# Load order of the late weights in a fused attention and feed-forward kernel: down weights ahead of output weights, gate weights split two and five

## The chip, the cores and the metric

The kernel runs on one core of a Trainium2 chip. The metric is the device time of one execution in microseconds (us), lower is better; times are medians over several runs.

## The reference

One transformer block with parallel branches over 2048 tokens of width 448: a layer norm, a sliding-window attention of 16 heads of 28 (window 256), a gated feed-forward of width 1792, and the sum of both with the input. All tensors are bf16.

```python
def _A_ref(x, wqkv, wo):
    qkv = (x @ wqkv).reshape(B, S, 3, H, Dh) ...            # H = 16, Dh = 28
    scores = einsum("bhqd,bhkd->bhqk", q, k) * Dh ** -0.5
    mask = (idx[:, None] - idx[None, :] >= 0) & (idx[:, None] - idx[None, :] < 256)
    p = softmax(where(mask, scores, -1e9))
    return einsum("bhqk,bhkd->bhqd", p, v) ... @ wo

def _B_ref(x, w_gate, w_up, w_down):
    return (gelu(x @ w_gate) * (x @ w_up)) @ w_down

xn = layernorm(x)
return x + _A_ref(xn, A_wqkv, A_wo) + _B_ref(xn, B_w_gate, B_w_up, B_w_down)
```

## The kernel before

**Tiling.** The tokens are cut into four query blocks of 512 (`qb` 0 to 3), each of four tiles of 128. For a block, `attention` runs the score steps (score matmuls into a PSUM tile of four banks, an exponential on ScalarE, masks, then the product with the values), and between the steps it runs pieces of other matmul work from a hand-written list, `plan`: projections of the next block, up-projections of this one, and the down and output projections of the block before (`gen_down`). After the attention steps of a block `gated` runs the feed-forward: the hidden width of 1792 is taken as seven pairs of 128 columns (pair p is columns 128p to 128p+127 of each half). For each pair `gate(p)` makes 14 matmuls into a PSUM tile `gt` of two banks and a GELU of 1024 columns on ScalarE (L539), `up(p)` makes the 14 matmuls of the up-projection, and `end(p)` multiplies both on VectorE (L546, L549) and calls `hook(2p)`. Block 0 makes the up-projection of pairs 0 to 4 ahead of time, in the attention steps, so that its `gated` runs gate 0 to 4, then gate 5, up 5, gate 6, up 6.

**PSUM.** The `gt` tiles are two buffers of two banks, the score tile `sc` of the next block is one buffer of all four of those banks. So the first score matmul of block 1 waits for the last GELU of block 0, and the second score step for the exponential of the first.

**Order.** The schedule is by hand: every engine runs its instructions in the order in which the code issues them. SyncE's queue (SP) issues nearly all DMAs. Eight DMA semaphores (HW0 to HW7, "lanes" below) are used in turn by the DMAs of SP and of ScalarE's queue, in program order. A DMA that is to use a lane first waits until the DMA that used it eight DMAs earlier has landed.

**The loads in question.** `ahead3` runs in the third score step of block 0. It issues, on SP, the copies `swap` and `swap_weights`, the gate weights `wg` with `load_ffn` (a load is two DMAs, one for each half of the partitions), the last two pairs of the up weights `wu`, the last four input tiles (`x_sb`, L827), the output weights `wo` in eight small DMAs (L831, L832) and the down weights `wd` in two large ones (L834). The last four rows of each head group in `wo` are laid out by `SLOTS`, since heads 14 and 15 travel in spare rows.

**What uses them.** `gate(p)` reads `wg`; `gen_down(0)`, in the attention steps of block 1, reads `wd` (L408) and later `wo` (L408, L417). The `wo` rows 64 to 127 of group 3 are a copy of rows 0 to 63, made on GpSimd (Pool) in `hook`. `hook` of block 0 also calls, at f = 8 (the end of pair 4), `o_collect(0, nc.scalar)`: three DMAs on ScalarE's own queue (L364) that take the attention output of heads 14 and 15 to DRAM, after Pool has written it (L622). At f = 0, 4, 8 and 10 it normalises an input tile (L170) and has SP transpose it by DMA (L184); at f = 12 `o_deliver` (L369) brings the rows back and Pool copies a part (L375).

Of the kernel before, what the change touches and what calls it, by code (L numbers as in the profile page):

```python
# [19 lines left out]
NF = F // P  # L20
# [7 lines left out]
def kernel(  # L28
# [11 lines left out]
    nc = tc.nc  # L40
# [26 lines left out]
    wg = const.tile([P, 7, F // 2], bf16, name="wg")  # L67
    wu = const.tile([P, 7, F // 2], bf16, name="wu")
    wd = const.tile([P, NF, D], bf16, name="wd")
    wo = const.tile([P, 4, D], bf16, name="wo")  # L70

    def rows(w, c0, n):
        return w[c0 * P:(c0 + n) * P, :].rearrange("(c p) n -> p c n", p=P)

    def load_ffn(dst, w, pairs):

        wv64 = w.rearrange("(c p) (h n) -> p c h n", p=64, h=2)
        ns = slice(pairs.start * P, pairs.stop * P)  # L80
        for hi in range(2):
            nc.sync.dma_start(out=dst[64 * hi:64 * hi + 64, :, ns], in_=wv64[:, :, hi, ns])
# [82 lines left out]
    def norm(t):  # L165
        xn = work.tile([P, 4, P], bf16, name="xn", bufs=4)
        xf = xn[:, :, :].rearrange("p a b -> p (a b)")
        both = ((0, D, 0), (D, 64, 384))
        for lo, n, src in both if t > 3 else both[:1]:
            nc.vector.tensor_scalar(out=xf[:, lo:lo + n], in0=x_sb[:, t, src:src + n], scalar1=mv_all[:, t, 0:1],  # L170
                                    scalar2=rstd_all[:, t:t + 1], op0=ALU.subtract, op1=ALU.mult)
        xns[t] = xn
# [9 lines left out]
    def dma_transp(t):  # L182

        nc.sync.dma_start_transpose(out=xnT[:, :, t * P:(t + 1) * P], in_=xns.pop(t)[:, :, :].rearrange("p a b -> p (a b)"))  # L184
# [103 lines left out]
    def fill_pads(last):  # L288


        def put(dst, src, n, lo):

            src = src.rearrange("p (j d) -> p j d", d=Dh)[:, :, lo:]
            if n == 4:
                nc.gpsimd.tensor_copy(out=dst[:, 12:16, Dh:32], in_=src[:, :, 24:28])
            src = src[:, :, 0:24].rearrange("p j (g i) -> p g j i", i=8)[:, :, :, 0:4]
            nc.gpsimd.tensor_copy(out=dst[:, 0:12, Dh:32].rearrange("p (g j) i -> p g j i", j=4), in_=src)

        if not last:
            for c in range(3):  # L300
                k = wraw[:, c, D + 12 * Dh:2 * D]
                put(wqp[:, c, :, :], k, 4, 0)
                put(wkp[:, c, :, :], k, 3, 4)
            return
        put(w3p[0:64, :, :], w3k[0:64, :], 4, 0)
        put(w3p[64:128, :, :], w3k[64:128, :], 3, 4)
        nc.gpsimd.memset(w3p[64:128, 12:16, :], 0.0)
# [163 lines left out]
    def new_hT(qb):  # L471
        hT = blk.tile([P, NF, QB], bf16, name="hT", tag="hT")
        hTs[qb] = hT

    def swap(qb, t=None, n=4):

        t0 = P * (4 * qb if t is None else t)
        to = t0 - qb * QB + ring(qb).start
        for hi in range(2):
            nc.sync.dma_start(out=xsw[64 * hi:64 * hi + 64, :, to:to + n * P],  # L480
                              in_=xnT[64 - 64 * hi:P - 64 * hi, 0:3, t0:t0 + n * P])

    def swap_weights():

        for hi, src in enumerate((wqp, wkp)):
            nc.sync.dma_start(out=wsq[64 * hi:64 * hi + 64], in_=src[64 - 64 * hi:P - 64 * hi, 0:3])
# [19 lines left out]
    def gen_up(qb, ps, shared=()):  # L506

        for p in ps:
# [9 lines left out]
            yield 330  # L518

    def gated(qb, early, last_v, flush, hook):  # L520

        hT = hTs[qb]
# [293 lines left out]
    def ahead3():  # L816
        for t in (5, 6, 7):
            norm(t)
            dma_transp(t)
        swap(1, 4, 2)  # L820
        fill_pads(False)
        swap_weights()
        swap(1, 6, 2)
        load_ffn(wg, B_w_gate, slice(0, 3))
        load_ffn(wg, B_w_gate, slice(3, 7))
        load_ffn(wu, B_w_up, slice(5, 7))
        nc.sync.dma_start(out=x_sb[:, 12:16, :], in_=xv[:, 12:16, :])  # L827
        wo_v = A_wo.rearrange("(g j d) n -> j d g n", g=4, j=4)
        tail = A_wo[14 * Dh:, :].rearrange("(t i) n -> i t n", i=4)
        for j, (t0, n) in enumerate(SLOTS):  # L830
            nc.sync.dma_start(out=wo[32 * j:32 * j + Dh, 0:n, :], in_=wo_v[j][:, 0:n])  # L831
            nc.sync.dma_start(out=wo[32 * j + Dh:32 * j + 32, 0:n, :], in_=tail[:, t0:t0 + n])  # L832
        for k in range(0, NF, 7):
            nc.sync.dma_start(out=wd[:, k:k + 7, :], in_=rows(B_w_down, k, 7))  # L834

    for qb in range(NB):
        if qb in (1, 3):
            tc.mark_branch_hint_location("general", hint="LikelyTaken",
                                         engines=[mybir.EngineType.DVE if qb == 1 else mybir.EngineType.PE])
        early = ()  # L840
        if qb == 0:
            new_hT(0)
            early = (0, 1, 2, 3, 4)
            def last_v():
                v_dense(2, pvs[2], False)
                v_copy(2, pvs[2], nc.vector.tensor_copy)

            u = chain(gen_qk(), gen_up(0, (1, 2, 3, 0, 4), (2, 3, 4)))
            w = gen_pairs(1, (("v", 0), ("v", 2), ("k", 0), ("k", 1), ("k", 2)))
            plan = [[last_v, lambda: stat(6), (u, 3), ahead], [(u, 2), ahead2, (u, 2)], [(u, 1), ahead3, (u, 7)], [(u, 8), lambda: stat(8)],  # L850
                    [lambda: stat(9), (u, 12), lambda: fill_pads(True)], [(u, 9), "sums"],
                    [(w, 7), "inverse", "scale", (w, 7), lambda: stat(10), (w, 3)],
                    [(w, 4), lambda: stat(11), lambda: rstd(8, 4), (w, 7), "masks", "sums", (w, 7), "inverse"]]
        else:
            d = gen_down(qb - 1)
            if qb < 3:
                u = gen_pairs(qb + 1, (("v", 0), ("k", 0), ("v", 2), ("k", 1), ("k", 2)))
                plan = [[(d, 14)], [(d, 11)], [(d, 11)], [(u, 7)], [(d, 17)], ["sums", (d, 1), (u, 7), "inverse"], [(u, 11)],
                        [lambda: q_last(qb + 1, nc.vector.tensor_copy), (d, 6), "sums"], [(d, 2), "inverse", (d, 9)],
                        [(u, 9), "masks", (u, 1)]]  # L860
                plan[3] = [(d, 1), (u, 7)]
                if qb == 2:
                    plan[0], plan[2] = [(d, 13)], [(d, 10)]
                if qb == 1:
                    for i, j in enumerate((0, 1, 2, 2)):
                        plan[j].insert(0, lambda t=12 + i: stat(t))
                    plan[4].append(lambda: rstd(12, 4))
                    plan[1] = plan[1][:1] + [lambda: q_last(1, nc.vector.tensor_copy), (d, 8)]
                    plan[2] = plan[2][:2] + [(d, 12), lambda: collect(1)]
                    plan[4].append(lambda: deliver(1))  # L870
            else:
                new_hT(3)
                early = (1, 2, 3, 4, 5, 6)
                u = gen_up(3, early, (4, 5, 6))
                plan = [[(u, 12)], [(u, 9)], [(d, 12)], [(d, 10)], [(d, 12)], [(d, 1), (u, 7), "sums"], [(d, 12), "inverse"],
                        ["sums", "inverse", (d, 11)], [(d, 11)], [(d, 1), "masks", (u, 13), "masks", (u, 1)]]
        if qb in (1, 2):
            swap(qb + 1)
        score_pool(1)
        rest, after, flush = attention(qb, plan)  # L880
        nc.scalar.preload_act_table(ACT.Gelu_apprx_tanh)
        score_pool(2)
        if qb not in hTs:
            new_hT(qb)

        def hook(f):
            after(f)
            if qb in (1, 2) and f == 0:
                collect(qb + 1)
            if f == (8, 2, 2, 0)[qb]:  # L890
                o_collect(qb, nc.sync if qb else nc.scalar)
            if f == (12, 4, 4, 0)[qb]:
                o_deliver(qb)
                o_finish(qb)
            if qb == 0 and f == 6:
                nc.gpsimd.tensor_copy(out=wo[64:128, 3, :], in_=wo[0:64, 3, :])
            if qb in (1, 2) and f == 10:
                deliver(qb + 1)
            t = ({0: 8, 4: 9, 8: 10, 10: 11} if qb == 0 else {4: 12, 6: 13, 8: 14, 10: 15} if qb == 1 else {}).get(f)
            if t is not None:  # L900
                norm(t)
                dma_transp(t)

        gated(qb, early, rest, flush, hook)
        if qb < NB - 1:
            nc.scalar.preload_act_table_set("natural_log_exp_and_others")
# [159 lines left out]
```

## Time and profile before

| | |
|---|---|
| median of 3 runs | 211.83 us (211.72 to 211.97) |
| the profiled execution | 211.66 us, its span 209.8 us |
| TensorE matmul (PE) busy | 205.4 us, 98% of the span |
| VectorE (DVE) busy | 156.4 us, 75% |
| ScalarE (ACT) busy | 134.7 us, 64% |
| GpSimd (POOL) busy | 44.0 us, 21% |
| DMA | 15.68 MB, 75 GB/s over the span |
| gate weights of block 0 first used | at 36.2 us |
| down weights first used | at 51.4 us |
| output weights first used by PE | at 58.5 us |

The profiled execution took 1.8 us more than its span; that part lies outside what the profile shows. All times below are microseconds from the span's start. Busy time of PE is modelled at the ends of matmuls, so a gap on PE is better read from the start times of its instructions.

### The profile page before, as it was taken

To read this page: it belongs to the slowest core of one execution; us is meant where nothing else is said; L and a number is where in the kernel's file an instruction comes from. 1 tells how busy PE (TensorE), PEld (TensorE's weight loads), DVE (VectorE), ACT (ScalarE), POOL (GpSimd) and SP (SyncE) were. 2 spreads that over 40 slices of the span, in tenths; PEclk is the share of its full clock that TensorE was granted. 3 is DMA by queue.
4 is the path that set the end of the run, shared out by engine and by line. 5 is a ranking of instruction groups with operands and counts; after the bars stand their busy time and mean duration, and the time that the engine had idled before them with its cause. 6 is when DMAs were issued, how large, how long until landed. Compare 5 with 4: busy or idle time off the path is not lost. (4 is left out here: it accounts for less than half of the span.)

```text
span 209.8 us, 6671 instructions
## 1 busy us (share of the span) xinstructions
PE 205.4 (98%) x2842; PEld 98.9 (47%) x2842; DVE 156.4 (75%) x359; ACT 134.7 (64%) x132; POOL 44.0 (21%) x87
## 2 busy tenths in 40 slices
PE   7999999999999999999999999999999999999994
PEld 2444444544454545444445444544444454544572
DVE  6898899899788984796438897395385699696532
ACT  4699896857677977423777787522587787756000
POOL 5389902260000220040000102012000022042000
PEclk9999999999999999999999999999999999999999
DMA  6999989969421001003321000100000010100011
GB/s 171 291 223 212 127 212 217 215 199 221 112 67 25 25 22 22 7 5 70 72 75 47 25 3 25 22 3 21 23 5 0 3 47 5 47 9 13 3 47 50
DMA packets 24890, 15.68 MB, mean 75 GB/s; under 512 B 9208, under 2 KB 24728, under 8 KB 24856
## 3 DMA queue, kind: packets, MB, share of 16 engines
q1 hardware_dynamic: 23814, 14.87, 31.2%
q10 hardware_dynamic: 1042, 0.34, 0.9%
q8 instruction: 23, 0.38, 0.8%
q14 instruction: 11, 0.09, 0.2%
HBM read 9.26 MB, written 2.41 MB: 56 GB/s over the span
## 5 line engine op out<-in xcount | busy, mean ns | idle before, releaser
L687 ACT ACTIVATE p_sb<-sc 128x2048 bf16<-128x2048 f32 x38 | 71.4, 1878 | 16.9 <-PE sc L682 11.9
L539 ACT ACTIVATE p_sb<-gt 128x1024 bf16<-128x1024 f32 x28 | 28.7, 1025 | 31.3 <-PE gt L499 30.2
L622 POOL TENSOR_TENSOR oN<-oc,l 128x512 bf16<-128x512 f32 x16 | 20.7, 1298 | 122.8 <-DVE l L635 122.8
L499 PE MATMUL gt<-xnT,wg 64*128 64x512 bf16 x224 | 45.6, 376 | 0.0
L408 PE MATMUL po<-wd,hT 128*128 128x448 bf16 (+1 forms) x224 | 44.7, 347 | 0.0
L499 PE MATMUL gt<-xsw,wg 64*128 64x512 bf16 x168 | 40.7, 376 | 0.0
L607 DVE TENSOR_TENSOR p_sb<-p_sb,masks 128x256 bf16<-128x256 bf16 (+1 forms) x98 | 30.9, 369 | 7.5 <-ACT p_sb L687 7.5
L549 DVE TENSOR_TENSOR hT<-p_sb,u 128x512 bf16<-128x512 bf16 x34 | 21.7, 675 | 13.4 <-PE u L499 13.3
L408 PEld LDWEIGHTS <-hT 128*128 128x128 bf16 x238 | 21.9, 98 | 19.1 <-issue 2.0
L499 PEld LDWEIGHTS <-wg 64*128 64x128 bf16 x392 | 19.0, 94 | 22.3
L499 PEld LDWEIGHTS <-wu 64*128 64x128 bf16 x392 | 19.1, 94 | 22.0 <-issue 0.7
L499 PE MATMUL u<-xnT,wu 64*128 64x512 bf16 x136 | 28.1, 376 | 0.0
L499 PE MATMUL u<-xsw,wu 64*128 64x512 bf16 x102 | 24.7, 376 | 0.0
L499 PE MATMUL ue<-xnT,wu 64*128 64x512 bf16 x88 | 18.1, 377 | 0.0
L641 DVE TENSOR_TENSOR oc<-oc,ov 128x512 f32<-128x512 f32 (+1 forms) x16 | 10.5, 659 | 9.8 <-ACT oc L639 9.6
L499 PE MATMUL ue<-xsw,wu 64*128 64x512 bf16 x66 | 16.2, 377 | 0.0
L682 PE MATMUL sc<-qT,kT 28*64 28x320 bf16 (+4 forms) x736 | 16.2, 259 | 0.0
L396 DVE TENSOR_TENSOR res<-po,x_sb 128x448 bf16<-128x448 f32 (+1 forms) x14 | 8.1, 606 | 7.9 <-PE po L408 6.7
L682 PEld LDWEIGHTS <-kT 28*64 28x64 bf16 x736 | 8.1, 103 | 12.2 <-issue 11.0
L516 DVE CAST hT<-ue 128x512 bf16<-128x512 f32 x16 | 10.6, 687 | 2.1 <-PE ue L499 2.0
L639 ACT COPY oc<-ov 128x512 f32<-128x512 f32 x16 | 9.4, 585 | 3.6 <-PE ov L656 3.6
L635 DVE STREAM_TRANSPOSE l<-inv_all 128x512 f32<-128x512 f32 x16 | 11.1, 701 | 0.1
(112 smaller groups left out, 256.6 us busy)
## 6 DMA issues: line engine op xcount, KB each, us to landing
out_dram<-res SPq DMA_DIRECT2D x15, 112.0 KB
wd<-in_B_w_down_dram SPq DMA_DIRECT2D x2, 784.0 KB
x_sb<-in_A_x_dram SPq DMA_DIRECT2D x3, 448.0 KB
xsw<-xnT SPq DMA_DIRECT2D x6, 192.0 KB
wu<-in_B_w_up_dram SPq DMA_DIRECT2D x4, 224.0 KB
wg<-in_B_w_gate_dram SPq DMA_DIRECT2D x2, 448.0 KB
wu<-in_B_w_up_dram SPq DMA_DIRECT2D x2, 336.0 KB
wg<-in_B_w_gate_dram SPq DMA_DIRECT2D x2, 336.0 KB
```

What stands on the lines that cost most here:

```text
L408: nc.tensor.matmul(po[:, 0:w], lhsT=x[:, k, tt * P:(tt + 1) * P], rhs=wt[:, k, lo:up], start=start and n == 0, stop=stop and n == len(term ...
L499: nc.tensor.matmul(ps, lhsT=w[64 * hi:64 * hi + 64, c, p * P:(p + 1) * P], rhs=xchunk(qb, hi, c, qb * QB, QB), start=c == 0, stop=c == 6, ...
L516: copy(out=hTs[qb][:, p + 7 * i, :], in_=us[i])
L539: nc.scalar.activation(out=ges[p][:, :, :], in_=gt[:, :, :], func=ACT.Gelu_apprx_tanh)
L549: nc.vector.tensor_tensor(out=hT[:, p + 7 * i, :], in0=ge[:, i, :], in1=u, op=ALU.mult)
L607: nc.vector.tensor_tensor(out=reg, in0=reg, in1=m, op=ALU.mult)
L622: nc.gpsimd.tensor_tensor(out=oN[:, g, :], in0=oc[:, :], in1=inv, op=ALU.mult)
L635: nc.vector.transpose(out=l1[:, :, :], in_=inv_all[:, 4 * qb + g, :].unsqueeze(2).to_broadcast([P, 16, 32]))
L639: nc.scalar.copy(out=oc[:, :], in_=ov[0][:, :])
L641: nc.vector.tensor_tensor(out=oc[:, q0:], in0=oc[:, q0:], in1=ov[1][:, q0:], op=ALU.add)
L682: nc.tensor.matmul(ss[k0:k0 + nk, j, col:col + nq], lhsT=kT[r, g, kt * P + k0:kt * P + k0 + nk], rhs=qT[r, g, ring(qb).start + q0:ring(qb) ...
L687: nc.scalar.activation(out=p_sb[:, :, 0:ncol], in_=ss[:, :, 0:ncol], func=ACT.Exp, scale=SCALE)
```

## The change

The gate weights are loaded as pairs 0 to 1 and pairs 2 to 6 instead of pairs 0 to 2 and 3 to 6. The two DMAs of the down weights are issued ahead of the eight of the output weights. The Pool copy within `wo` is issued at f = 10 instead of f = 6.

```diff
-        load_ffn(wg, B_w_gate, slice(0, 3))
-        load_ffn(wg, B_w_gate, slice(3, 7))
+        load_ffn(wg, B_w_gate, slice(0, 2))
+        load_ffn(wg, B_w_gate, slice(2, 7))
         load_ffn(wu, B_w_up, slice(5, 7))
         nc.sync.dma_start(out=x_sb[:, 12:16, :], in_=xv[:, 12:16, :])
+        for k in range(0, NF, 7):
+            nc.sync.dma_start(out=wd[:, k:k + 7, :], in_=rows(B_w_down, k, 7))
         wo_v = A_wo.rearrange("(g j d) n -> j d g n", g=4, j=4)
         tail = A_wo[14 * Dh:, :].rearrange("(t i) n -> i t n", i=4)
         for j, (t0, n) in enumerate(SLOTS):
             nc.sync.dma_start(out=wo[32 * j:32 * j + Dh, 0:n, :], in_=wo_v[j][:, 0:n])
             nc.sync.dma_start(out=wo[32 * j + Dh:32 * j + 32, 0:n, :], in_=tail[:, t0:t0 + n])
-        for k in range(0, NF, 7):
-            nc.sync.dma_start(out=wd[:, k:k + 7, :], in_=rows(B_w_down, k, 7))
...
-            if qb == 0 and f == 6:
+            if qb == 0 and f == 10:
                 nc.gpsimd.tensor_copy(out=wo[64:128, 3, :], in_=wo[0:64, 3, :])
```

On SP's queue, from the load of the last input tiles to the first DMA transpose of the next block, the rows before are these (a row is one DMA with its line, what it writes and reads, its shape, and the lanes and engines that it waits for; the lane that it waits for is the one that it then uses):

```order
L827 DMA x_sb<-in_A_x_dram 128x4x448 [waits DMAHW0_49]
L831 DMA wo<-in_A_wo_dram 28x4x448 [waits DMAHW1_49,PE_49]
L832 DMA wo<-in_A_wo_dram 4x4x448 [waits DMAHW2_49]
L831 DMA wo<-in_A_wo_dram 28x4x448 [waits DMAHW3_49]
L832 DMA wo<-in_A_wo_dram 4x4x448 [waits DMAHW4_49]
L831 DMA wo<-in_A_wo_dram 28x3x448 [waits DMAHW5_49]
L832 DMA wo<-in_A_wo_dram 4x3x448 [waits DMAHW6_49]
L831 DMA wo<-in_A_wo_dram 28x3x448 [waits DMAHW7_49]
L832 DMA wo<-in_A_wo_dram 4x3x448 [waits DMAHW0_49]
L834 DMA wd<-in_B_w_down_dram 128x7x448 [waits DMAHW1_49]
L834 DMA wd<-in_B_w_down_dram 128x7x448 [waits DMAHW2_49]
L184 DMA_TRANSPOSE xnT<-xn 128x4x128 [waits DMAHW3_49,DVE_49]
```

On the same queue at the same place, the rows of the changed kernel are these:

```order
L827 DMA x_sb<-in_A_x_dram 128x4x448 [waits DMAHW0_49]
L829 DMA wd<-in_B_w_down_dram 128x7x448 [waits DMAHW1_49]
L829 DMA wd<-in_B_w_down_dram 128x7x448 [waits DMAHW2_49]
L833 DMA wo<-in_A_wo_dram 28x4x448 [waits DMAHW3_49,PE_49]
L834 DMA wo<-in_A_wo_dram 4x4x448 [waits DMAHW4_49]
L833 DMA wo<-in_A_wo_dram 28x4x448 [waits DMAHW5_49]
L834 DMA wo<-in_A_wo_dram 4x4x448 [waits DMAHW6_49]
L833 DMA wo<-in_A_wo_dram 28x3x448 [waits DMAHW7_49]
L834 DMA wo<-in_A_wo_dram 4x3x448 [waits DMAHW0_49]
L833 DMA wo<-in_A_wo_dram 28x3x448 [waits DMAHW1_49]
L834 DMA wo<-in_A_wo_dram 4x3x448 [waits DMAHW2_49]
L184 DMA_TRANSPOSE xnT<-xn 128x4x128 [waits DMAHW3_49,DVE_49]
```

The two `wd` rows have moved ahead of the eight `wo` rows, and each `wo` DMA now has a lane two further on: lanes HW5, HW6 and HW7 belonged to the fifth, sixth and seventh `wo` DMA and now belong to the third, fourth and fifth. From the transposes on the lanes are as before.

On ScalarE, from the last copy of attention output of block 0 (L639) to the first exponential of block 1 (L687), the rows are the same before and after; L539 is a GELU, L364 is one of the three DMAs of `o_collect`, L906 loads the function table of the exponential:

```order
L639 COPY oc<-ov 128x512 [waits PE_49,Pool_49]
L539 ACTIVATE p_sb<-gt 128x1024 [waits PE_49] x4
L364 DMA o_130<-oN 28x512 [waits DMAHW5_49,Pool_49]
L364 DMA o_130<-oN 16x512 [waits DMAHW6_49]
L364 DMA o_130<-oN 12x512 [waits DMAHW7_49]
L539 ACTIVATE p_sb<-gt 128x1024 [waits DVE_49,PE_49,Activation_49]
L539 ACTIVATE p_sb<-gt 128x1024 [waits DVE_49,PE_49]
L906 ACT_TABLE_LOAD
L687 ACTIVATE p_sb<-sc 128x2048 [waits DVE_49,PE_49,Activation_49]
```

No row moved here, but the lanes HW5, HW6 and HW7 that the three DMAs wait for are held by other `wo` DMAs than before. On PE the order of instructions is the same too; the wait for the second load of gate weights now stands at the first weight load of gate 2 instead of gate 3, and the first `wo` matmul waits for one lane more. On Pool the order is the same: between f = 6 and f = 10 it has no other instruction.

## Prediction

> **What bounds the kernel now.** I read the page's engine totals first, then the waits, then the order of time on SP, ACT and PE around the moved loads. The page and the waits (waiter, releaser, total, times, longest) say:
>
> ```profile
> PE 205.4 (98%) x2842; PEld 98.9 (47%) x2842; DVE 156.4 (75%) x359; ACT 134.7 (64%) x132; POOL 44.0 (21%) x87
> PEld L682 <- issue: 11.0, 29, 0.4
> PEld L333 <- DMA xsw<-xnT: 0.2, 1, 0.2
> ```
>
> PE is busy for 205.4 of 209.8 us. What it is short of is mostly its own issue between kinds of matmul (29 times, never over 0.4 us); of the DMAs the rows show one wait of 0.2 us. So no load that is moved here is late today, and a gain has almost nothing to come from. What the change can do is make something late. I look for the nearest edges. On PE, around the end of block 0 and the first steps of block 1:
>
> ```profile
> 40.39 0.59 PE L499 MATMUL gt<-xsw,wg 64*128 64x512 bf16 x2
> ...
> 51.05 0.42 PE L682 MATMUL sc<-qT,kT 28*64 28x320 bf16 x16
> 51.41 2.82 PE L408 MATMUL po<-wd,hT 128*128 128x448 bf16 x14
> 54.16 0.43 PE L682 MATMUL sc<-qT,kT 28*64 28x320 bf16 x24
> ```
>
> 40.39 is the start of gate 2, 51.05 the first score step of block 1, 51.41 the first use of `wd`, 54.16 the second score step. On SP, the issue of the loads (start, duration with any wait in the queue):
>
> ```profile
> 31.62 2.94 SPq L827 DMA_DIRECT2D x_sb<-in_A_x_dram  x1
> 34.66 2.20 SPq L831 DMA_DIRECT2D wo<-in_A_wo_dram  x1
> ...
> 39.12 0.32 SPq L831 DMA_DIRECT2D wo<-in_A_wo_dram  x1
> 40.24 0.25 SPq L832 DMA_DIRECT2D wo<-in_A_wo_dram  x1
> 41.13 0.32 SPq L831 DMA_DIRECT2D wo<-in_A_wo_dram  x1
> 42.61 0.25 SPq L832 DMA_DIRECT2D wo<-in_A_wo_dram  x1
> 42.91 1.00 SPq L834 DMA_DIRECT2D wd<-in_B_w_down_dram  x2
> 45.71 6.69 SPq L184 DMA_TRANSPOSE xnT<-xn  x4
> ...
> SPq L831 <- DMA wg<-in_B_w_gate_dram: 1.2, 1, 1.2
> SPq L832 <- DMA x_sb<-in_A_x_dram: 1.1, 1, 1.1
> SPq L832 <- DMA wu<-in_B_w_up_dram: 0.8, 1, 0.8
> SPq L831 <- DMA wu<-in_B_w_up_dram: 0.6, 1, 0.6
> ```
>
> The fifth to eighth `wo` DMA each wait for the lane of an earlier load, so their starts tell when those landed: the last of `wg` at 39.12, the two of `wu` at 40.24 and 41.13, `x_sb` at 42.61, in the order of issue. `x_sb` alone took 2.94 us to be issued, with no wait named: the queue was full. What is issued behind these loads is moved behind them.
>
> **The change, part by part.**
>
> *The down weights.* They may now be issued from 34.66 on, as the queue takes them, and move once `x_sb` has landed at 42.61. Sizes, and the rate of DMA in single microseconds (the last two columns are the DMA share and GB/s):
>
> ```profile
> wd<-in_B_w_down_dram SPq DMA_DIRECT2D x2, 784.0 KB
> x_sb<-in_A_x_dram SPq DMA_DIRECT2D x3, 448.0 KB
> wo<-in_A_wo_dram SPq DMA_DIRECT2D x2, 98.0 KB
> wo<-in_A_wo_dram SPq DMA_DIRECT2D x2, 14.0 KB
> ...
> 36.00:37.00 1.00, 1.00 (x12) 0.58 (x10) 1.00 (x4) 1.00 (x3) 0.00 (x0) 1.00 1.20 218
> 38.00:39.00 1.00, 1.00 (x74) 0.85 (x63) 0.64 (x2) 0.68 (x2) 0.22 (x1) 1.00 1.15 238
> 39.00:40.00 1.00, 1.00 (x12) 0.43 (x10) 0.70 (x2) 1.00 (x2) 1.00 (x1) 1.00 1.15 343
> 41.00:42.00 1.00, 1.00 (x12) 0.49 (x10) 1.00 (x3) 0.61 (x1) 0.00 (x0) 1.00 0.26 62
> 46.00:47.00 1.00, 1.00 (x12) 0.48 (x10) 1.00 (x2) 0.15 (x1) 0.69 (x1) 1.00 1.09 379
> 48.00:49.00 1.00, 1.00 (x12) 0.43 (x10) 1.00 (x3) 0.24 (x1) 0.00 (x0) 1.00 1.14 391
> ```
>
> The two `wd` DMAs are 1568 KB, 1.61 MB. At the mean of their own rate (385 GB/s, from 379 and 391) they take 4.2 us; at the pace of `x_sb` (448 KB from 41.13 to 42.61, 303 KB a us) 5.2 us. So `wd` lands at 46.8 to 47.8. PE wants it at 51.41 and does not wait for it today: gain nothing.
>
> *The output weights.* They now land behind `wd`. The third `wo` DMA lands after 98 + 14 + 98 = 210 KB more, 0.55 to 0.7 us: at 47.35 to 48.5. PE wants `wo` only in the first third of block 1's steps, some ten microseconds on. But ScalarE's queue waits for it: the first DMA of `o_collect` uses the lane HW5, which the fifth `wo` DMA held before (issued at 39.12, landed long ago) and the third holds now. Behind it in ACT's order stand the GELU of gate 5, that of gate 6, the table load and the first exponential of block 1:
>
> ```profile
> 45.68 1.42 ACTq L364 DMA_DIRECT2D o<-oN  x3
> 47.22 1.02 ACT L539 ACTIVATE p_sb<-gt 128x1024 bf16<-128x1024 f32 x1 [1.07 <-POOL wo L896]
> 49.66 1.02 ACT L539 ACTIVATE p_sb<-gt 128x1024 bf16<-128x1024 f32 x1 [1.41 <-PE gt L499]
> 50.70 1.28 ACT L906 ACT_TABLE_LOAD   x1
> 51.99 1.88 ACT L687 ACTIVATE p_sb<-sc 128x2048 bf16<-128x2048 f32 x1
> ...
> 44.38 1.26 POOL L622 TENSOR_TENSOR oN<-oc,l 128x512 bf16<-128x512 f32 x1 [0.36 <-DVE l L635]
> 45.71 0.98 POOL L896 COPY wo<-wo 64x448 bf16<-64x448 bf16 x1
> ```
>
> Today `o_collect` starts at 45.68, when Pool's L622 is done (44.38 + 1.26 = 45.64). From that start to the end of the GELU of gate 5 it is 47.22 + 1.02 - 45.68 = 2.56 us. The GELU of gate 6 starts at 49.66 for PE's sake, so a start of `o_collect` up to 49.66 - 2.56 = 47.10 costs nothing. From there on GELU, table load and exponential have no gap between them, and the exponential ends at 51.99 + 1.88 = 53.87; the second score step, which needs the one score buffer, starts at 54.16. That is at most 0.29 us more. So from 47.10 to 47.39 on, each microsecond of lateness is one on PE, which never makes it up, since it is busy to the end.
>
> The middle of 47.35 and 48.5 is 47.9: 0.5 us past 47.39. The ends: nothing (47.35 is before it) and 1.4 us (48.5 against 47.10). I take 0.5 us, with the middle, since the row of `wd` itself speaks for the fast end and the landing of the load just ahead of it for the slow one.
>
> *The gate weights.* The bytes of both loads together are the same, so the second ends at 39.12 as before; it is now wanted by gate 2 (40.39, its weights some 0.2 us earlier) instead of one gate later. 1.1 us of cover: nothing. The shorter first load frees nobody, since no row has PE waiting for `wg`.
>
> *Pool's copy.* Its place in Pool's order is the same (nothing stands between f = 6 and f = 10), so the edit as such does nothing; what moves it is the lanes it waits for, from 45.71 to about 48. Its successor on Pool is far off:
>
> ```profile
> 55.23 0.40 POOL L375 COPY oN<-oN 64x256 bf16<-64x256 bf16 x1 [8.54 <-DMA oN<-o]
> 45.60 1.64 DVE L546 TENSOR_TENSOR hT<-p_sb,hT 128x1024 bf16<-128x1024 bf16 x2
> 47.68 1.28 DVE L546 TENSOR_TENSOR hT<-p_sb,hT 128x1024 bf16<-128x1024 bf16 x2
> ```
>
> Beside the copy two products of VectorE took 1.64 us, without it 1.28: the 0.36 us are lost two microseconds later instead. Nothing, at most 0.4 either way on DVE, which PE does not wait for by more than that.
>
> *The transposes.* The first now waits on SP for the first `wo` DMA (lane HW3), until about 47.5 instead of 45.71. Four of them and their waits took 6.69 us, to 52.40. At worst they end a microsecond or two later; behind them on SP is `o_deliver`, whose rows Pool copies at 55.23 and PE uses some 3 us after that. That cover hides it; gone, it would cost what exceeds 3 us.
>
> *Waits on PE.* Two more lane waits, at gate 2 and at the first `wo` matmul. Each existing one took 51 ns:
>
> ```profile
> L408 PEldq EVENT_SEMAPHORE  x9: 51/51/51, 51.1 to 198.4; - x9
> ```
>
> Between nothing and 0.1 us together; I take nothing, since they stand in the sequencer, ahead of the matmuls.
>
> *Sum.* 211.66 us of the profiled execution plus 0.5 is 212.16. The median of the runs is 0.17 us above that execution, so I forecast 212.3 us.
>
> **The rivals.**
>
> *It is absorbed: 211.8 us.* In the row 41 to 42 DMA moved only 62 GB/s although `x_sb` landed at 42.61: most of it was there by 41, and a small part trailed by some 1.6 us. If `wo` does not depend on that trailing part, or it catches up, `wd` and three `wo` DMAs follow from 41 on: 41 + 4.2 + 0.55 is 45.8, and `o_collect` starts as it does today. For it: the trailing part would have bandwidth to itself at the end. Against: four landings in a row, 39.12 to 42.61, keep their distance. [...]
>
> *DMA is slower there: 215 us.* If `wd` moves at the pace of the gate weights (228 GB/s, the mean of 218 and 238) it takes 7.0 us and the three `wo` DMAs 0.95: 50.6, 3.2 us past 47.39. Against: the rows from 39 on (343, 379, 391) are of the same shape of load.
>
> *Gate 2 waits: 212.6 us.* If the longer rows of the second load move worse, and it lands after 40.2 instead of 39.12, PE stands at gate 2. The second load has 224 KB more; if the shorter first load gives nothing back, that is 1.0 us at 228 GB/s, 40.1, just in time; 2 us would cost 0.8.
>
> *Something gets faster: 211.2 us.* Earlier `wd` would help if PE waited for it; no row says so.
>
> **How the numbers follow.** The forecast has 0.50 and spans 211.8 to 213.2 (0 to 1.4 us over the median); 0.2%, about what a measurement of this kernel can tell from no change, is 0.42 us, and about a quarter of this case lies below it (0.13). Absorbed 0.32, slow DMA 0.08, gate 2 0.05, faster 0.05. Slower: 0.37 + 0.08 + 0.05 = 0.50. Same: 0.13 + 0.32 = 0.45. Faster: 0.05. The range, 211.7 to 213.3, takes in the absorbed case and all of the forecast; left out are slow DMA and faster.
>
> **What would show it.** Right: in ACT's order of time L364 starts at 47.4 to 48.5 instead of 45.68, the second GELU after it starts later than 49.66, and PE has a gap ahead of the second score step (54.16) and none before. Wrong: L364 still starts by 47.1 (absorbed); a gap on PE at gate 2; PE waiting for `wd` or `wo` itself; or a delay on VectorE that reaches PE at 51.41 first.

## The result and the profile after

The changed kernel is slower. Its median is 213.39 us (22 runs, 211.79 to 216.13), that of the kernel before in the same comparison 211.88 us (22 runs, 211.60 to 214.28). The ratio of the runs that the comparison keeps is 1.0051, with a 95% interval of 1.0028 to 1.0073. The profiled execution took 212.00 us, its span is 210.3 us (211.66 and 209.8 before): it is one of the fastest runs of this kernel, so its rows show the least of the loss. Two more profiles of the same kernel are among the experiments.

The engine totals of the page hardly differ:

```profile
PE 205.1 (98%) x2837; PEld 98.8 (47%) x2842; DVE 156.1 (74%) x359; ACT 134.6 (64%) x132; POOL 44.4 (21%) x87
```

PE's order of time at the same places (gate 2, the first score step, the first use of `wd`, the second score step):

```profile
40.41 0.59 PE L499 MATMUL gt<-xsw,wg 64*128 64x512 bf16 x2
...
51.42 0.42 PE L682 MATMUL sc<-qT,kT 28*64 28x320 bf16 x16 [0.27 <-ACT p_sb L539]
51.78 2.82 PE L408 MATMUL po<-wd,hT 128*128 128x448 bf16 x14
54.61 0.43 PE L682 MATMUL sc<-qT,kT 28*64 28x320 bf16 x24
```

Gate 2 stands where it stood (40.39). The first score step is at 51.42 instead of 51.05 and now waits, for a GELU on ScalarE; the second is at 54.61 instead of 54.16. So 0.37 us are lost at the first and 0.08 more at the second, 0.45 in all, and PE keeps that to the end: it is nearly the whole difference of the two spans (210.3 against 209.8). Behind it stands ScalarE's queue:

```profile
47.76 1.54 ACTq L364 DMA_DIRECT2D o<-oN  x3
49.43 1.94 ACT L539 ACTIVATE p_sb<-gt 128x1024 bf16<-128x1024 f32 x2 [3.26 <-DVE xn L170]
51.39 1.28 ACT L906 ACT_TABLE_LOAD   x1
52.68 1.88 ACT L687 ACTIVATE p_sb<-sc 128x2048 bf16<-128x2048 f32 x1
```

`o_collect` starts at 47.76 instead of 45.68, and the two GELUs, the table load and the exponential follow without a gap, 0.7 us late. (The releaser that the row names, L170, is not it: the GELU starts at 49.43, behind the three DMAs ahead of it in the queue, which end at 49.30.) The wait for the first lane, HW5, is an instruction of its own on this queue, and is over at 47.4, before at 45.1; `o_collect` itself starts almost 0.4 us behind it:

```profile
L364 ACTq EVENT_SEMAPHORE  x1: 17/17/17, 47.4 to 47.4; - x1
```

On SP the reason:

```profile
32.69 5.81 SPq L829 DMA_DIRECT2D wd<-in_B_w_down_dram  x2
...
43.70 0.32 SPq L833 DMA_DIRECT2D wo<-in_A_wo_dram  x1
46.90 0.25 SPq L834 DMA_DIRECT2D wo<-in_A_wo_dram  x1
47.24 6.26 SPq L184 DMA_TRANSPOSE xnT<-xn  x4
...
SPq L834 <- DMA wd<-in_B_w_down_dram: 2.9, 1, 2.9
```

The seventh and the eighth `wo` DMA wait for the lanes of the two halves of `wd`: these landed by 43.70 and 46.90. The first transpose waits for the first `wo` DMA, and starts at 47.24; `o_collect` waits for the third. DMA by microseconds (the last column is GB/s):

```profile
40.00:41.00 1.00, 1.00 (x12) 0.50 (x10) 0.97 (x3) 1.00 (x3) 0.07 (x1) 1.00 1.16 395
43.00:44.00 1.00, 1.00 (x12) 0.49 (x10) 0.93 (x3) 0.51 (x2) 1.00 (x1) 1.00 1.09 376
...
45.00:46.00 1.00, 1.00 (x12) 0.43 (x10) 1.00 (x2) 0.85 (x1) 0.68 (x1) 1.00 0.65 154
46.00:47.00 1.00, 1.00 (x12) 0.49 (x10) 1.00 (x3) 0.17 (x1) 0.00 (x0) 1.00 0.15 44
```

Most of `wd` and `wo` has moved by 46, at 355 to 395 GB/s from 40 to 44 us and less behind; in the microsecond in which the second half of `wd` lands, DMA moves 44 GB/s. A small part trails, and the waits are for that part. The trace has it step by step: in it the semaphore of a lane rises in sixteen steps for a load of 128 rows and in fourteen for one of 28. For the second half of `wd` ten steps are done by 44.60 us and the last comes at 46.88; for the third `wo` DMA thirteen are done by 46.63 and the last comes at 47.37. The rest is as harmless as reckoned: Pool's copy is late (47.60, before 45.71), the rows brought back are copied a microsecond later (56.35, before 55.23), and no row of PE waits for either.

```profile
47.60 1.44 POOL L896 COPY wo<-wo 64x448 bf16<-64x448 bf16 x1 [1.93 <-DMA wo<-in_A_wo_dram]
56.35 0.40 POOL L375 COPY oN<-oN 64x256 bf16<-64x256 bf16 x1 [7.30 <-DMA oN<-o]
```

### The profile page after: what moved, and what is told of

Same layout as the page of the kernel before. It is cut to its first block, busy times and chain, and to the rows that moved or that the text cites. A ratio compares the mean times of both kernels' runs of the same rounds, so it can differ in the third digit from the quotient of the medians.

```text
span 210.3 us, 6668 instructions
## 1 busy us (share of the span) xinstructions
PE 205.1 (98%) x2837; PEld 98.8 (47%) x2842; DVE 156.1 (74%) x359; ACT 134.6 (64%) x132; POOL 44.4 (21%) x87
## 5 line engine op out<-in xcount | busy, mean ns | idle before, releaser
L687 ACT ACTIVATE p_sb<-sc 128x2048 bf16<-128x2048 f32 x38 | 71.4, 1878 | 16.7 <-PE sc L682 12.5
L539 ACT ACTIVATE p_sb<-gt 128x1024 bf16<-128x1024 f32 x28 | 28.6, 1025 | 32.1 <-PE gt L499 28.8
L639 ACT COPY oc<-ov 128x512 f32<-128x512 f32 x16 | 9.4, 586 | 3.6 <-PE ov L656 3.6
```

What stands on the lines that cost most here:

```text
L539: nc.scalar.activation(out=ges[p][:, :, :], in_=gt[:, :, :], func=ACT.Gelu_apprx_tanh)
L639: nc.scalar.copy(out=oc[:, :], in_=ov[0][:, :])
L687: nc.scalar.activation(out=p_sb[:, :, 0:ncol], in_=ss[:, :, 0:ncol], func=ACT.Exp, scale=SCALE)
```

## The experiments

Theory A is that of the prediction: ScalarE's `o_collect` waits for lanes of output weights that land behind the down weights. G is that gate 2 waits for the larger second load, S that SyncE's transposes and what follows them are late.

**The gate split alone.**

```diff
-        load_ffn(wg, B_w_gate, slice(0, 3))
-        load_ffn(wg, B_w_gate, slice(3, 7))
+        load_ffn(wg, B_w_gate, slice(0, 2))
+        load_ffn(wg, B_w_gate, slice(2, 7))
```

> The kernel before with the gate weights split two and five, nothing else. Theory A (ScalarE's three o_collect DMAs wait for output weights that now land behind the down weights, and the GELUs, the table load and the exponential behind them are late): the loads behind the gate weights are as before, so ratio 0.998 to 1.002 and o_collect at 45.7 us. Theory G (gate 2 waits for the larger second load in part of the runs): all of the loss is here, ratio 1.003 to 1.007, with a gap on PE ahead of 40.4 us. Theory S (the transposes and what follows on SyncE are late): as A, 1.000.

Ratio 1.0003 (0.9976 to 1.0030), median 211.81 us. G falls. In its profile PE runs later for reasons ahead of the change (0.34 us at 14 us, 0.66 us at the GELU of gate 4), and `o_collect` by as much; relative to the GELU ahead of it (45.12 and 45.68 before) it starts as before:

```profile
45.78 1.02 ACT L539 ACTIVATE p_sb<-gt 128x1024 bf16<-128x1024 f32 x1 [0.49 <-PE gt L499]
46.34 1.41 ACTq L364 DMA_DIRECT2D o<-oN  x3
```

**The down weights alone.** The kernel before, with the loop over `wd` moved ahead of the loop over `wo`:

```diff
+        for k in range(0, NF, 7):
+            nc.sync.dma_start(out=wd[:, k:k + 7, :], in_=rows(B_w_down, k, 7))
         for j, (t0, n) in enumerate(SLOTS):
...
-        for k in range(0, NF, 7):
-            nc.sync.dma_start(out=wd[:, k:k + 7, :], in_=rows(B_w_down, k, 7))
```

> The kernel before with the two down-weight loads issued ahead of the output weights, the gate weights and the Pool copy as before. Theory A: the whole loss, ratio 1.003 to 1.008, o_collect starts at 47 to 49 us and the second GELU behind it later than 49.7. Theory G: 1.000. Theory S: the whole loss as well, but with PE waiting for transposed input or weights rather than for ScalarE.

Ratio 1.0053 (1.0027 to 1.0080): the whole loss. Its profile (215.58 us, the longest of its twelve runs) shows the same chain and something more. ScalarE:

```profile
45.57 1.02 ACT L539 ACTIVATE p_sb<-gt 128x1024 bf16<-128x1024 f32 x1 [0.49 <-PE gt L499]
49.72 1.56 ACTq L364 DMA_DIRECT2D o<-oN  x3
```

PE:

```profile
53.39 0.42 PE L682 MATMUL sc<-qT,kT 28*64 28x320 bf16 x16 [1.82 <-ACT p_sb L539]
53.74 4.50 PE L408 MATMUL po<-wd,hT 128*128 128x448 bf16 x14
```

And the stretches behind the wait (the column ahead of the last two is the granted clock):

```profile
55.00:56.00 1.00, 1.00 (x4) 0.46 (x3) 0.98 (x2) 1.00 (x1) 0.00 (x0) 0.50 0.54 108
56.00:57.00 1.00, 1.00 (x4) 0.39 (x3) 0.62 (x3) 0.53 (x1) 0.00 (x0) 0.50 0.18 41
```

After a wait of 1.82 us the clock falls to 0.50, and the 14 matmuls take 4.50 us instead of 2.82: the wait costs 1.7 us more than itself.

**Half of the down weights ahead.** The changed kernel, with the second half of `wd` loaded behind `wo`:

```diff
-        for k in range(0, NF, 7):
-            nc.sync.dma_start(out=wd[:, k:k + 7, :], in_=rows(B_w_down, k, 7))
+        nc.sync.dma_start(out=wd[:, 0:7, :], in_=rows(B_w_down, 0, 7))
...   (the loop over wo)
+        nc.sync.dma_start(out=wd[:, 7:14, :], in_=rows(B_w_down, 7, 7))
```

> The changed kernel, but only the first of the two down-weight loads is ahead of the output weights, the second is behind them. Theory A: the output weights land about 2.1 us earlier than in the changed kernel (half of 1.6 MB at 385 GB/s), so o_collect starts by 46.5 us, inside the 47.1 to 47.4 us that costs nothing: ratio 1.000, at most 1.002. Theory G: the loss stays, 1.003 to 1.007. Theory S: about the same as the changed kernel, since all transposes stand behind the same bytes.

Ratio 0.9996 (0.9973 to 1.0019). `o_collect` starts at 45.81, and the first score step waits for nothing:

```profile
45.81 1.71 ACTq L364 DMA_DIRECT2D o<-oN  x3
```

```profile
51.18 0.42 PE L682 MATMUL sc<-qT,kT 28*64 28x320 bf16 x16
51.54 3.09 PE L408 MATMUL po<-wd,hT 128*128 128x448 bf16 x14
```

The first matmuls on `wd` took 3.09 us instead of 2.82: in the trace the first one that needs the second half, now the last load, starts at 52.77 instead of the 52.49 that its place in the row would give, when the load's lane makes its last step at 52.73. So 0.3 us are lost there in this profile; the ratio does not show them.

**`o_collect` taken off ScalarE.** The changed kernel, all loads as changed:

```diff
-                o_collect(qb, nc.sync if qb else nc.scalar)
+                o_collect(qb, nc.sync if qb else nc.gpsimd)
```

> The changed kernel with the three o_collect DMAs of block 0 issued from GpSimd instead of ScalarE; all loads as changed. Theory A: ScalarE waits for no load any more, the GELUs start when PE is done, ratio 0.998 to 1.002, and the PE gaps at 51 and 55 us are gone although the weights land as late as before. Theories G and S: the loss stays, 1.003 to 1.007.

Ratio 1.0015 (0.9991 to 1.0039), median 212.20 us. The weights are as late as in the changed kernel, or later:

```profile
46.55 1.84 POOL L364 DMA_DIRECT2D o<-oN  x3 [0.30 <-POOL oN L622]
49.26 0.66 POOL L896 COPY wo<-wo 64x448 bf16<-64x448 bf16 x1 [0.87 <-DMA wo<-in_A_wo_dram]
```

In block 1 PE waits for nothing but its own issue (it runs 0.6 us later from 20 us on, as in the kernel with the gate split alone):

```profile
51.65 0.42 PE L682 MATMUL sc<-qT,kT 28*64 28x320 bf16 x16
52.00 2.82 PE L408 MATMUL po<-wd,hT 128*128 128x448 bf16 x14
54.76 0.43 PE L682 MATMUL sc<-qT,kT 28*64 28x320 bf16 x24
```

On GpSimd's queue the three DMAs start at 46.55, ahead of the landing of `wo`, for which Pool's copy waits until 49.26: so the edit takes away the wait for the lane along with ScalarE's queue. The transposes are as late as ever (the first starts at 48.73), and nothing waits for them. So the late weights cost through ScalarE's queue and not otherwise: S falls. Some 0.4 us of the median over the kernel before (211.79 in this comparison) are left, inside the interval; what they are was not found.

**A larger dose.** The changed kernel with one more half of `wd`, into a dead buffer, ahead of `wo`:

```diff
+        spare_w = wraw[...]                                 # 128 x 7 x 448, no longer read
+        nc.sync.dma_start(out=spare_w, in_=rows(B_w_down, 0, 7))
```

> The changed kernel with one more load of 784 KB (the first half of the down weights again, into a dead buffer) between the down weights and the output weights. Theory A: the output weights land 2.1 us later (0.80 MB at 385 GB/s), so ScalarE and PE wait 2.1 us longer than in the changed kernel, whose runs are 1.5 us over the kernel before: 3.6 us, ratio 1.017; and if a wait of PE of about 2 us also brings the half clock that followed the 1.82 us wait in the profile of the down weights alone (some 3.4 us at 0.5, 1.6 us more), up to 1.025. Theory S: the transposes are 2.1 us later as well, but they have several microseconds of cover, so no more than the changed kernel, 1.007.

Ratio 1.0240 (1.0208 to 1.0273), median 217.22 us.

```profile
45.46 1.02 ACT L539 ACTIVATE p_sb<-gt 128x1024 bf16<-128x1024 f32 x1 [0.49 <-PE gt L499]
52.08 1.40 ACTq L364 DMA_DIRECT2D o<-oN  x3
```

```profile
55.59 0.66 PE L682 MATMUL sc<-qT,kT 28*64 28x320 bf16 x16 [4.12 <-ACT p_sb L539]
56.17 5.34 PE L408 MATMUL po<-wd,hT 128*128 128x448 bf16 x14
...
57.00:58.00 1.00, 1.00 (x4) 0.35 (x3) 1.00 (x3) 1.00 (x1) 0.00 (x0) 0.50 0.32 65
```

The wait grows to 4.12 us, and the half clock is there too (0.50 in the last row): 5.34 us for the 14 matmuls. Cause and effect scale.

**Two more profiles of the changed kernel.**

> The changed kernel once more, for a second profile. Theory A with a landing that varies from run to run: a time between 212 and 214.5, and the PE wait ahead of the first or second score step of block 1 accounts for the excess over 211.7 (0.3 to 2.5 us), the start of o_collect later than 47.4 us by the same amount; clock 1.0 unless the wait is near 2 us.

> The same kernel a third time, with the same expectation: the later o_collect starts, the longer the PE wait, one for one. Were it another cause, PE's wait would stand at another place or not follow the start of o_collect.

They took 214.57 and 212.92 us. The first look, ScalarE and PE:

```profile
46.55 1.02 ACT L539 ACTIVATE p_sb<-gt 128x1024 bf16<-128x1024 f32 x1 [0.49 <-PE gt L499]
50.41 1.46 ACTq L364 DMA_DIRECT2D o<-oN  x3
```

```profile
53.99 0.42 PE L682 MATMUL sc<-qT,kT 28*64 28x320 bf16 x16 [1.43 <-ACT p_sb L539]
```

The second look:

```profile
45.20 1.02 ACT L539 ACTIVATE p_sb<-gt 128x1024 bf16<-128x1024 f32 x1 [0.49 <-PE gt L499]
48.72 1.39 ACTq L364 DMA_DIRECT2D o<-oN  x3
```

```profile
52.22 0.42 PE L682 MATMUL sc<-qT,kT 28*64 28x320 bf16 x16 [1.01 <-ACT p_sb L539]
```

The GELU of gate 4 (45.12 in the kernel before, first row of each ScalarE fence) tells how late PE was already, for reasons ahead of the change. With that taken off, five profiles line up:

| profile | `o_collect` starts | PE late at the first score step | difference |
|---|---|---|---|
| changed kernel | 47.73 | 0.34 | 47.4 |
| second look | 48.64 | 1.09 | 47.6 |
| first look | 48.98 | 1.51 | 47.5 |
| down weights alone | 49.27 | 1.89 | 47.4 |
| larger dose | 51.74 | 4.20 | 47.5 |

(GELU 4 of the changed kernel was at 45.15.) Every microsecond past 47.4 to 47.6 is one on PE. The first look has a second loss, 1.4 us at about 31 us, which is the subject of the last experiment.

**Gate weights split one and six.** The kernel before with `slice(0, 1)` and `slice(1, 7)`.

> The kernel before with the gate weights split one and six: the second load is wanted one gate earlier still, at 38.7 us, and should land at 38.1 to 39.1 us as ever. If the cover was reckoned rightly (1.1 us at gate 2, 1.5 us less at gate 1) PE waits 0 to 0.4 us ahead of gate 1: ratio 1.000 to 1.002. If the longer rows moved worse, the wait would be 1 us or more, ratio 1.005 and up, and gate 2 would be at risk in the changed kernel as well.

Ratio 1.0005 (0.9989 to 1.0022), median 212.15 us against 211.89. In the profile gate 1 does wait:

```profile
39.87 0.39 PE L499 MATMUL gt<-xsw,wg 64*128 64x512 bf16 x2 [0.60 <-DMA wg<-in_B_w_gate_dram]
```

The second load was there at 39.8, later than the 38.1 to 39.1 that was expected, in an execution that was on time at gate 0 (36.26, before 36.24). What PE loses is more than the idle time of that row: gate 2 stands at 41.39 instead of 40.39, and the span is a microsecond longer (210.8 against 209.8).

```profile
41.39 0.38 PE L499 MATMUL gt<-xsw,wg 64*128 64x512 bf16 x2
```

So one gate earlier the cover is gone, and this profile stands at the upper case of the expectation, though the ratio of the runs does not. Gate 2, whose weights are wanted at some 40.2, would have had 0.4 us left here and not 1.1.

**ScalarE's chain made longer.** The kernel before, no load moved, with three or six short copies between the last GELU of block 0 and the table load:

```diff
             nc.scalar.activation(out=ges[p][:, :, :], in_=gt[:, :, :], func=ACT.Gelu_apprx_tanh)
+            if not qb and p == 6:
+                for _ in range(3):                          # or 6
+                    nc.scalar.copy(out=scr[:, :], in_=x_sb[:, 0, 0:D // 2])
```

> The kernel before with three short copies on ScalarE (224 columns each, some 0.4 us, into a scratch tile) between the last GELU of block 0 and the table load, no load moved. Theory A (the gap between the exponential's end and the second score step is at most 0.29 us, all beyond it is lost on PE): PE waits 1.2 - 0.29 = 0.9 us ahead of the second score step, ratio 1.004, clock 1.0 throughout. If ScalarE's chain had more cover than that: 1.000.

> As the kernel with three copies, with six: PE waits 2.4 - 0.29 = 2.1 us ahead of the second score step. Without a change of the clock that is ratio 1.010. If a wait of this length brings the half clock for 3.4 us (theory C), 1.6 us more in all or some of the runs: up to 1.0175, with a granted clock of 0.5 in the microseconds behind the wait.

Three copies: ratio 1.0063 (1.0035 to 1.0090), median 0.89 us over the kernel before.

```profile
50.48 1.19 ACT L543 COPY scr<-x_sb 128x224 bf16<-128x224 bf16 x3
51.68 1.28 ACT L910 ACT_TABLE_LOAD   x1
```

```profile
54.91 0.43 PE L686 MATMUL sc<-qT,kT 28*64 28x320 bf16 x24 [0.77 <-ACT p_sb L691]
```

Six: ratio 1.0145 (1.0095 to 1.0196) in four runs; its profiled execution had also lost 1.9 us at 31 us.

```profile
52.66 2.42 ACT L543 COPY scr<-x_sb 128x224 bf16<-128x224 bf16 x6
55.09 1.28 ACT L910 ACT_TABLE_LOAD   x1
```

```profile
58.32 0.43 PE L686 MATMUL sc<-qT,kT 28*64 28x320 bf16 x24 [2.00 <-ACT p_sb L691]
```

```profile
59.00:60.00 1.00, 1.00 (x7) 0.46 (x6) 0.96 (x4) 1.00 (x1) 0.00 (x0) 1.00 0.15 39
```

Copies of 1.19 and 2.42 us give waits of 0.77 and 2.00 us. Reckoned from the first score step (50.96 and 53.14 here, 51.05 before), the table load is 1.07 and 2.30 us later than before, and the second score step 0.84 and 2.07: the chain has 0.23 us of cover, inside the 0.29 expected, without any load being late.

Theory C is that a wait of this length brings the half clock. In the profile with six copies it does not: the clock stayed at 1.00 behind a wait of 2.00 us. But two of the other three runs (215.72 and 215.41 us) have a mean granted clock of 0.992, as the profile of the down weights alone has, and that makes 1.7 us; the one without (213.75 us, clock 1.00) is 1.9 us over the kernel before. So in some runs the half clock probably came; no trace shows where.

**The wait at 31 us.** Six of the thirteen profiles have a wait of PE for the swapped input copy `xsw`: 0.2 us in four of them, among these the kernel before and the changed one, and more in the first look and in the kernel with six copies:

```profile
PEld L333 <- DMA xsw<-xnT: 1.4, 1, 1.4
```

```profile
PEld L334 <- DMA xsw<-xnT: 1.9, 1, 1.9
```

It comes ahead of the loads that were changed. The kernel before, with that copy issued earlier:

```diff
-        swap_weights()
         swap(1, 6, 2)
+        swap_weights()
```

> The kernel before with one change elsewhere: the copy of the last two swapped input tiles (xsw, the second swap of tile pair 6) is issued on SyncE ahead of the two swapped weight copies (wsq) instead of behind them. PE waited for this copy at L333, 0.2 us in the profile before and 1.9 us in one of the experiments. If that wait is what lifts single runs of every kernel by some 1.6 us, it is gone: lowest run 0.1 to 0.2 us lower and fewer runs above 213, ratio 0.997 to 1.000. If the swapped weights are then late instead, PE waits at L347, 1.000 or more.

Ratio 0.9990 (0.9972 to 1.0009), median 211.90 against 211.96 us: its profile has no such wait, but no gain is shown. That this wait is what lifts single runs stays open.

## Why the prediction was right, and where it was not

**Right: the mechanism, and the place but for one step.** PE was the bound, no moved load was late before, nothing could be gained, and the loss enters through the three `o_collect` DMAs on ScalarE. That is shown from both sides: taken off ScalarE the wait is gone with the weights as late as ever, and with half or one and a half times the weights ahead the loss goes or grows. The threshold of 47.10 to 47.39 us was 47.4 to 47.6 in five profiles. The place was off by one step: the prediction has the gap ahead of the second score step and none before, and it stands ahead of the first, with only 0.08 us more at the second. The working passed over the first step's own wait, for the GELU of gate 6: before, that GELU ends at 50.68 and the step starts at 51.05; after, at 51.37 and 51.42. So of the 0.37 us between them 0.32 can go, little more than the 0.24 between the exponential and the second step (53.87 and 54.16 before, 54.56 and 54.61 after), and the late GELU comes first.

**Mis-sized: when `o_collect` can start.** The term was the landing of the third `wo` DMA, 47.35 to 48.5, with 47.9 taken and 0.5 us of loss. The profiled execution of the changed kernel fits it (47.76, 0.45 us). But in the three profiles of that kernel `o_collect` starts at 47.7, 48.6 and 49.0, each taken relative to PE, and the median of the runs is 1.5 us over the kernel before, three times the forecast; the ratio of 1.0051 makes it 1.1 us, twice the forecast. The median of 213.39 us is just above my range (up to 213.3), the ratio within it. That the forecast fits the profiled execution so well is luck: it is one of the fastest.

Two things failed in the step from rates to a start. First, the two rates gave the ends of the landing, while the rows show the bulk moving as fast as its own earlier row (355 to 395 GB/s, the fast end) and landing set by a small part that trails, differently in each run. In the first look the last step of the second half of `wd` comes 2.3 us behind the one before it (49.52 and 47.25). I had seen that part at 41 to 42 us and used it only for the rival. Second, I took the landing for the start. The lane of the third `wo` DMA makes its last step at 47.37, 48.33 and 50.02 in the changed kernel, the second look and the first, and `o_collect` starts at 47.76, 48.72 and 50.41: 0.39 us behind each time, a term that the sum put at nothing. What ScalarE's queue does in that time no row shows. A half clock on top, as in the profile of the down weights alone, was not in the sum at all.

**The rivals.** *Absorbed* fails: the bulk was there by 46 as that rival has it, and `wo` waited for the trailing part all the same. In the microsecond in which `wd` lands 44 GB/s were moved, and the eighth `wo` DMA, which waits for the lane of its second half, starts at 46.90, just behind the last of the sixteen steps (46.88). That `wo` depends on the trailing part, the lanes show: in the first look the third `wo` DMA, of 28 rows, has thirteen of its fourteen steps by 48.15 and the last at 50.02, while the fourth, of 4 rows and issued behind it, has made its four steps by 48.27. *Slow DMA* fails with 355 to 395 GB/s. *Gate 2* did not wait in any profile of the changed kernel; the cover is not always the 1.1 us that was reckoned, since with the split one and six the second load was there at 39.8 only.

**The small terms.** Pool's copy, the transposes, and the waits on PE cost nothing that shows, as reckoned: the transposes end about 1 us later and nobody waits. That the queue was full while `x_sb` was issued was my reading of its 2.94 us; the rows fit it: the two `wd` DMAs took 1.00 us to issue at 42.91 before, and 5.81 us at 32.69 in the changed kernel, behind the other loads.

## What to carry to other kernels

The three DMAs on ScalarE's queue made ScalarE's later work wait for what they waited for, here a shared semaphore whose former user is an unrelated load: the GELU of gate 6, the table load and the exponential were 0.7 us late in the changed kernel's profile, and with the DMAs on GpSimd's queue the wait was gone. Before loads are reordered, it pays to count which DMA stands eight places ahead of each such issue. With PE busy for 98% of the span and waiting 0.2 us for DMAs, a reordering of loads has next to nothing to gain, and what it can lose is read from the few tenths of a microsecond between ScalarE's chain and the matmul that needs its buffer. The time at which a load landed here was set by its slowest part and varied by more than a microsecond between runs (`o_collect` at 47.73 to 48.98 in three profiles of one kernel, taken relative to PE), so cover should be counted against that and not against the mean rate; and from the landing to the start of the DMA that waited for it another 0.39 us went by in each of the three.

## What was not expected of the hardware

A wait of PE of 1.82 us, in the profile of the down weights alone, was followed by about 3.4 us at half the clock (0.67, 0.50, 0.50 and 0.62 in the four microseconds from 54 on), which cost 1.7 us. With the larger dose, whose wait was 4.12 us, the half clock came before the wait was over and lasted about 6.8 us (0.75 in the microsecond from 54 on, 0.50 in the next six, 0.84 in the one from 61 on).

Three other waits ahead of the first two score steps brought none. Behind the 2.00 us of the kernel with six copies and the 1.43 us of the first look the clock stayed at 1.00 in every microsecond up to 62 and 58 us. In the second look, with 1.01 us, the mean clock of the whole execution is 1.00, and the 14 matmuls behind the wait took 2.82 us, as before.

So the length of the wait alone does not tell: 1.82 us brought the half clock, and 2.00 us did not. What decides it is not shown by these runs. With waits of some two microseconds the loss at this place was the wait itself in one profile (2.00 us) and the wait and 1.7 us more in another (1.82 us).
